# Attention scores as whole float32 products on 64x64 tiles of TensorE, with keys and queries unsplit

## The chip, the cores and the metric

One core of a Trainium2 chip runs the whole program. The metric is the device time of one execution in microseconds; the kernel before was run three times (667.96, 668.06 and 671.06, median 668.06). Lower is better. A profile of one execution lies beside the times; all rows in this document come from such profiles.

## The reference

Four batches of eight heads, 768 tokens, head size 64. Each query attends to the 31 keys around it (distance under 16) and to 24 summaries, one for each block of 32 tokens: of the keys the maximum, of the values the mean. A block's score gets log(32) added. Then comes a feed-forward layer over all heads' outputs. Inputs and outputs are float32 (the weights arrive as 8-byte floats).

```python
k_sum = k.reshape(B, H, nb, 32, D).max(axis=3)
v_sum = v.reshape(B, H, nb, 32, D).mean(axis=3)
scores_l = np.where(abs(i - j) < 16, q @ k.T / 8, -1e9)
scores_s = q @ k_sum.T / 8 + np.log(32)
a = softmax(concat([scores_l, scores_s]))
x = a @ concat([v, v_sum])            # then (tokens, 512)
h = x @ w_in                          # (512, 2048)
out = (h - np.tanh(h)) @ w_out        # (2048, 512)
```

## The kernel before

The work is cut into eight **passes** u = 0 to 7: half a batch's sequence each, 384 queries of all eight heads. Within a pass heads go in four **pairs** p, and the 384 queries in three **tiles** of 128. The attention of a pass feeds its feed-forward part: `moe_in` (line 1071, tiles pH, 12 matmuls for each of 16 slices f of the hidden size) and `moe_out` (line 1136, tiles pY0 to pY2). Both split float32 into a high and a low float32r part and use three matmuls for one; only `moe_out` of pass 0 uses whole float32. A loop over slots (from line 1185 on) lists the steps of all stages: attention runs 22 slots ahead of the feed-forward part, so scores of a later pass stand between pH and pY steps of the one before.

What is listed there is not the order that runs. Each step is a task with a cost for each engine that could take it, the tiles it reads and writes, and a due time; a planner (`schedule`, line 172) simulates the engines and writes one fixed order for each. The tables BIAS, KB and SL move due times by hand. Where the planner sees TensorE idle in the first 100 us it puts dummy matmuls on the identity matrix (`keep_warm`, line 1279, tile pX).

Scores before (`prep` line 781, `scores` line 926):
- Passes 0 and 1 load q and k in rows of 64 numbers, turn them on TensorE (three transposes of q, four of k, in even passes two more for the rest of the keys: "q turn", "k turn", "top turn"), copy them into a line that holds each tile's keys with the 24 block maxima between them, and multiply in whole float32. One half of q per head stands in rows that are zero for the other head, so a tile is four matmuls of 128 rows by 64 columns of the array, 118 columns each (24 summaries and 94 keys), two of them on the left and two on the right half of the array's columns.
- Passes 2 to 7 load q and k as 32x32 blocks, turn them on DVE, split both into high and low parts ("q high", "q low", "q again", "k high", "k low", "k again", "top put"), and make a tile with three float32r matmuls over the whole array:

```python
tensor.matmul(o, at(qh)[:, qs], at(kx[1])[:, :, ws], start=True, stop=False)
for a in range(2):
    tensor.matmul(o[:, a], at(qa[a])[:, qs], at(kx[0])[:, a, ws], start=False, stop=a == 1)
```

After the scores come, tile by tile, a minimum with the mask added ("min", DVE), exponentials (ACT), sums and inverses (DVE) and the scaling; the probabilities are turned (on TensorE in passes 0 and 1, "p turn"; on DVE and through a scratch tensor in the others) and multiplied with the values ("values", 118 rows). Weights come from DRAM into three places of `raw` and are made into float32 on ACT, DVE and POOL (`convert`, line 564). After pass 0 the w_out weights are split too (`split_whole`, line 617) into tiles whose earlier use has ended (`homes`, line 490).

In the trace a float32 matmul stands as two instructions, a float32r matmul and a transpose as one; so a row of a timeline says x4 for two float32 matmuls of the order.

Of the kernel before, what the change touches and what calls it, by code (L numbers as in the profile page):

```python
# [31 lines left out]
WHOLE = 2  # L32

WIDE = 2

MASKED = 0

# [5 lines left out]

KB = {('chunk load', 0): -1261, ('chunk load', 2): 12, ('chunk sum', 0): 636, ('chunk sum', 2): 272, ('const', 0): 183, ('const', 2): -383, ('exp', 0): 297, ('exp', 1): 82, ('exp', 2): -892, ('g', 0): 113, ('g', 1): 66, ('g', 2): 493, ('g high', 1): -379, ('g high', 2): -2162, ('g low', 1): 208, ('g low', 2): 450, ('in', 0): 83, ('in', 1): 8, ('in', 2): -53, ('in part', 2): 226, ('inverse', 0): -566, ('inverse', 1): 1, ('inverse', 2): 770, ('k again', 1): -661, ('k again', 2): -3493, ('k high', 0): 72, ('k high', 1): -374, ('k high', 2): 27, ('k line', 2): -53, ('k load', 0): 397, ('k load', 1): -478, ('k load', 2): 1488, ('k low', 1): -538, ('k low', 2): 636, ('k turn', 0): 300, ('k turn', 1): 34, ('k turn', 2): -325, ('mask split', 2): 129, ('mean copy', 0): 194, ('mean out', 0): -352, ('mean out', 1): -301, ('mean out', 2): -105, ('mean put', 0): 21, ('mean put', 1): 858, ('mean put', 2): 1756, ('mean turn', 0): 376, ('mean turn', 1): -106, ('mean turn', 2): -121, ('min', 0): -122, ('min', 1): 10, ('min', 2): -569, ('normal', 0): 892, ('normal', 1): 313, ('normal', 2): -714, ('out', 0): -471, ('out', 1): -414, ('out', 2): 232, ('p load', 2): 753, ('p out', 0): -129, ('p out', 1): -250, ('p out', 2): 11, ('p save', 2): 740, ('p turn', 0): 40, ('p turn', 1): -180, ('p turn', 2): -212, ('pad', 2): -517, ('pad line', 2): -248, ('pair', 2): 767, ('q again', 1): 38, ('q again', 2): -982, ('q half', 2): -38, ('q high', 0): 669, ('q high', 1): 151, ('q high', 2): -623, ('q load', 0): -366, ('q load', 1): -882, ('q load', 2): 224, ('q low', 1): -548, ('q low', 2): -1311, ('q turn', 0): 656, ('q turn', 1): 183, ('q turn', 2): 51, ('scores', 0): -77, ('scores', 1): -60, ('scores', 2): -6, ('seen', 2): 2487, ('seen max', 2): 1706, ('seen turn', 2): 2079, ('series', 0): 493, ('series', 1): 269, ('series', 2): 349, ('square', 0): 337, ('square', 1): 369, ('square', 2): -674, ('sum', 0): 506, ('sum guard', 0): -45, ('sum guard', 1): -677, ('sum guard', 2): 572, ('tanh', 0): 284, ('tanh', 1): -121, ('tanh', 2): -2026, ('top high', 1): -46, ('top high', 2): -83, ('top line', 2): -207, ('top low', 0): -194, ('top low', 1): -1742, ('top low', 2): -16, ('top max', 0): 144, ('top max', 1): -1138, ('top max', 2): -179, ('top put', 0): -72, ('top put', 1): -846, ('top put', 2): 1034, ('top turn', 0): 154, ('top turn', 1): 15, ('top turn', 2): -3, ('v load', 0): 442, ('v load', 1): -277, ('v load', 2): 100, ('values', 0): -7, ('values', 1): 332, ('values', 2): 456, ('w high part', 0): -51, ('w high part', 1): -1591, ('w high part 2', 0): 399, ('w high part 2', 1): -325, ('w high part 2', 2): -1898, ('w join', 0): 115, ('w join', 1): -38, ('w join', 2): -129, ('w load', 0): 82, ('w load', 1): 468, ('w low', 0): 305, ('w low', 1): -1539, ('w low part', 0): -737, ('w low part', 1): -253, ('w low part 2', 1): -210, ('w low part 2', 2): -1956, ('w scale', 0): 312, ('w scale', 1): -761, ('w sign', 0): 121, ('w sign', 1): -283, ('w sign', 2): -119, ('x high', 0): 248, ('x high', 1): -248, ('x high', 2): 502, ('x low', 0): -591, ('x low', 1): 232, ('x low', 2): 259, ('y out', 2): -505, ('y store', 2): 1285, ('x whole', 2): 34, ('pick', 2): 18, ('big', 1): -123, ('direct', 1): 24, ('cube', 2): -140, ('w shift', 0): -153, ('sum out', 0): -33, ('big', 2): 18, ('top pre', 0): 17, ('pick', 1): -55, ('pick', 0): 21, ('direct', 0): -139, ('cube', 0): 30, ('cube', 1): -7, ('big', 0): 97, ('w sign 2', 0): 34, ('w sign 2', 1): 17, ('w shift', 1): -15}

HALF = {'const': (12, 12), 'k load': (8, 16), 'v load': (18, 36), 'chunk load': (8, 8), 'chunk sum': (8, 8), 'q load': (12, 15), 'w load': (9, 32), 'w scale': (8, 32), 'w shift': (8, 32), 'w low': (7, 32), 'w sign': (3, 20), 'w join': (3, 20), 'w high part': (3, 26), 'w low part': (3, 26), 'w sign 1': (4, 12), 'w sign 2': (4, 12), 'top pre': (16, 16), 'top turn': (4, 8), 'top max': (8, 16), 'top put': (14, 20), 'q turn': (6, 9), 'k turn': (6, 9), 'q high': (4, 8), 'k high': (8, 16), 'sum': (8, 8), 'sum out': (8, 8), 'scores': (17, 25), 'mean turn': (2, 4), 'mean out': (2, 4), 'mean copy': (8, 8), 'mean put': (0, 10), 'min': (32, 50), 'exp': (32, 50), 'sum guard': (15, 25), 'inverse': (15, 25), 'normal': (30, 49), 'p turn': (15, 24), 'p out': (15, 24), 'values': (14, 24), 'x high': (4, 8), 'x low': (4, 8), 'top high': (0, 4), 'top low': (0, 4), 'in': (3, 19), 'tanh': (2, 18), 'square': (3, 18), 'cube': (2, 18), 'series': (2, 18), 'g': (2, 17), 'big': (2, 17), 'direct': (2, 17), 'pick': (2, 17), 'out': (2, 45), 'w high part 2': (3, 6), 'w low part 2': (0, 6), 'g high': (0, 11), 'g low': (0, 10), 'q low': (0, 2), 'q again': (0, 2), 'k low': (0, 2), 'k again': (0, 2), 'y out': (0, 0), 'y store': (0, 0)}


def phase(t):
# [27 lines left out]
HELD = {"pair", "mean copy", "w join", "w shift", "w low", "w sign", "w low part", "w low part 2", "w low part 3", "w high part", "w high part 2", "w scale", "normal", "g high", "g low", "q low", "k low", "g", "cube", "big", "k again", "q again", "top pre"}  # L77
HELD_LATE = {"q high", "k high"}


def holds(t):
    return t.kind in HELD or t.kind in HELD_LATE and phase(t) == 2

# [238 lines left out]
def program(  # L322
# [24 lines left out]
    NG = H // HG  # L347
    PG = HG // 2
    WIN = 15
    SC = 64 + NB + 94  # L350
    N2 = SC - 64
    KS = P + NB
    KC = 3 * KS + P
# [647 lines left out]
    def transpose_probs(u, p, i, tag):  # L1001
# [16 lines left out]
        if i < NT - 1:  # L1018
            return
# [301 lines left out]
```

## Time and profile before

| | |
|---|---|
| median of three runs | 668.06 us (667.96 to 671.06) |
| profiled execution | span 667.8 us, from the first to the last instruction; the list of runs has no separate time for it |
| granted TensorE clock, mean | 0.998 |
| PE, DVE, ACT, POOL busy | 654.8, 473.4, 459.8, 266.7 us |
| DMA | 73.09 MB, mean 109 GB/s |

The page gives busy time by engine and 40 slices of the span; the windows give the same for chosen stretches; a timeline lists instructions of one engine by start. A matmul's shown length contains the time in which it drains, so what a step costs is read from start to start.

### The profile page before, as it was taken

How to read it: one execution, taken by the hardware profiler on the slowest of the kernel's cores; microseconds unless marked ns; L12 is line 12 of the kernel's file. 1: busy time of each engine (PE TensorE's matmuls, PEld its weight loads, DVE VectorE, ACT ScalarE, POOL GpSimd, SP SyncE). 2: the span in 40 equal slices, each digit the busy share in tenths (PEclk: the TensorE clock that was granted, in tenths of full speed). 3: DMA queues.
4: the chain of work that ended last, by engine and by line, in shares of the span. 5: the costliest groups of instructions: out<-in, count | busy, mean ns of one | idle time of the engine just before them, and what ended most of it. 6: DMA issues, size and time to landing. Idle time of an engine off the chain costs nothing.

```text
span 667.8 us, 13029 instructions
## 1 busy us (share of the span) xinstructions
PE 654.8 (98%) x4109; PEld 564.3 (84%) x4109; DVE 473.4 (71%) x1414; ACT 459.8 (69%) x1342; POOL 266.7 (40%) x354
## 2 busy tenths in 40 slices
PE   8999999999999999999999999999999999999997
PEld 6775665788998989899988988898998989898995
DVE  3998889899998889549876799678785875222222
ACT  4997899878885878557883878667765875343332
POOL 4334133146543565335542444544433642122221
PEclk9999999999999999999999999999999999999999
DMA  9897866663245655334244745534252413200001
GB/s 210 231 265 208 216 188 204 144 105 96 71 90 121 151 124 119 76 80 119 60 101 95 161 95 108 121 76 112 60 127 45 108 48 80 61 16 32 1 0 51
DMA packets 165393, 73.09 MB, mean 109 GB/s; under 512 B 131048, under 2 KB 155592, under 8 KB 165320
## 3 DMA queue, kind: packets, MB, share of 16 engines
q1 hardware_dynamic: 164520, 72.02, 44.6%
q8 instruction: 34, 0.56, 0.4%
q10 hardware_dynamic: 800, 0.20, 0.2%
q14 instruction: 39, 0.32, 0.2%
HBM read 54.39 MB, written 15.73 MB: 105 GB/s over the span
## 4 chain that ended last, share of the span: by engine, by line
PE 81%; DVE 8%; ACT 4%; DMA 3%; issue 1%; POOL 0%; SPq 0%; ACTq 0%; DVEq 0%
PE pY L69 37%; PE pH L69 36%; PE pS L69 4%; PE pX L69 2%; PE pT L69 2%; DMA raw<-in_moe_w_out_dram 2%; DVE raw L69 1%; DVE probw L69 1%; DVE k L69 1%; ACT probw L69 1%; ACT gu L69 1%; DMA tmp<-in_v_dram 1%; DVE wf L69 1%; DMA rawq<-in_q_dram 1%; DVE vacc L69 1%
## 5 line engine op out<-in xcount | busy, mean ns | idle before, releaser
L69 PE MATMUL pH<-xh,w 128*128 128x384 f32 x1024 | 268.4, 343 | 0.7 <-POOL w L69 0.5
L69 POOL TENSOR_TENSOR gu<-gu,gt 128x384 f32<-128x384 f32 x112 | 118.1, 1054 | 234.7 <-ACT gu L69 161.6
L69 PEld LDWEIGHTS pH<-xh,w 128*128 128x128 f32 x1024 | 185.7, 188 | 12.5 <-issue 3.3
L69 PE MATMUL pY<-wf,gh 128*128 128x512 f32 x411 | 169.1, 442 | 1.1 <-DVE gh L69 1.1
L69 PE MATMUL pH<-xl,w 128*128 128x384 f32 x448 | 151.8, 339 | 0.0
L69 ACT ACTIVATE gu<-pH 128x384 f32<-128x384 f32 x128 | 62.5, 488 | 106.7 <-PE pH L69 62.7
L69 ACT ACTIVATE prob<-prob,stats 128x182 f32<-128x182 f32 x217 | 93.3, 442 | 36.3 <-DVE stats L69 33.6
L69 PEld LDWEIGHTS pY<-wf,gh 128*128 128x128 f32 x411 | 76.4, 189 | 25.6 <-issue 14.0
L69 DVE CAST gh<-gu 128x384 fp32r<-128x384 f32 x60 | 25.6, 426 | 84.7 <-POOL gu L69 78.6
L69 PEld LDWEIGHTS pH<-xl,w 128*128 128x128 f32 x448 | 84.1, 188 | 0.0
L69 POOL TENSOR_TENSOR gl<-gu,gh 128x384 fp32r<-128x384 f32 x59 | 63.7, 1082 | 35.7 <-DVE gh L69 13.0
L69 ACT ACTIVATE gu<-gu 128x384 f32<-128x384 f32 x128 | 66.9, 522 | 0.5
L69 ACT ACTIVATE gt<-pH 128x384 f32<-128x384 f32 x128 | 61.5, 481 | 2.2 <-PE pH L69 1.9
L69 DVE CUSTOM_DVE_ANT_0 prob<-pS,mask 128x182 f32<-128x182 f32 x144 | 47.1, 340 | 10.5 <-PE pS L69 8.4
L69 PE MATMUL pY<-vsum,gh 128*128 128x512 f32 x126 | 50.1, 398 | 0.0
L69 PE MATMUL pY<-vsum,gl 128*128 128x512 f32 x126 | 49.8, 395 | 0.0
L69 DVE TENSOR_TENSOR k<-raw,k 64x384 fp32r<-64x384 f32 x96 | 46.4, 522 | 1.0
L69 DVE STREAM_TRANSPOSE turned<-prob 128x384 f32<-128x384 f32 x72 | 41.3, 573 | 5.8 <-ACT prob L69 4.5
L69 PE MATMUL pS<-k,q 128*128 128x364 f32 (+1 forms) x208 | 37.8, 295 | 0.9 <-DVE stats L69 0.4
L69 PEld LDWEIGHTS pS<-k,q 128*128 128x128 f32 (+1 forms) x208 | 29.4, 173 | 9.3 <-issue 4.0
L69 DVE TENSOR_TENSOR gl<-gu,gh 128x384 fp32r<-128x384 f32 x53 | 31.2, 589 | 7.0 <-ACT gh L69 3.4
L69 DVE TENSOR_SCALAR raw<-raw 128x512 uint32<-128x512 uint32 (+1 forms) x53 | 33.1, 648 | 3.3 <-DMA raw<-in_moe_w_in_dram 1.9
(185 smaller groups left out, 1185.2 us busy)
## 6 DMA issues: line engine op xcount, KB each, us to landing
place<-turned SPq DMA_DIRECT2D x96, 96.0 KB
probT<-place SPq DMA_DIRECT2D x24, 384.0 KB
raw<-in_moe_w_in_dram SPq DMA_DIRECT2D x16, 512.0 KB
raw<-in_moe_w_out_dram SPq DMA_DIRECT2D x16, 512.0 KB
out_dram<-tmp SPq DMA_DIRECT2D x23, 256.0 KB
rawq<-in_q_dram SPq DMA_DIRECT2D x96, 48.0 KB
raw<-in_k_dram SPq DMA_DIRECT2D x48, 96.0 KB
vw<-in_v_dram SPq DMA_DIRECT2D x40, 96.0 KB
```

What stands on the lines that cost most here:

```text
L69: return lambda *args, **kwargs: self._tc.keep_in_program_order(op(*args, **kwargs))
```

## The change

Scores of all passes become whole float32 products of the unsplit q and k, on quarters of the array: 64 rows (one head of the pair) by 64 columns (one half of a tile's queries). A pair's three tiles are now one step of 24 matmuls, for each tile four on the 24 summaries and four on the 94 keys around (79 at the sequence's ends); head 0 goes to bank pS, head 1 to pT (pY0 in pass 0). The scale -1/8 moves into the "min", masked places get the opposite sign, and the softmax of a pair is one step. In the value tiles the means now stand in rows 0 to 23 and the values behind them.

For that k of batch 0 is loaded in rows of six tokens and q of pass 0 in rows of three. Turning a pair's keys takes 24 transposes on two row halves (once for both passes, kept in a new tile kT), and q of pass 0 six. All steps that split q and k or put summaries between keys are gone, and with them the zero fills and pads. `homes` starts with kT (six split weights), then rawq1, vw1, vsum1 and vsum0. The tables that move due times are new, so nearly every step stands elsewhere.

The core of the diff:

```diff
     def load_k(b, g):
...
-        for h in range(HG):
-            dma("k load", lambda e, h=h: e.dma_start(tile()[:, :, h], k[b, HG * g + h].rearrange("(c r) d -> r c d", c=6)), S * D * 4, D * 4, w=[keys[h]])
+        for m in range(PG):
+            hs = slice(HG * g + 2 * m, HG * g + 2 * m + 2)
+            dma("k load", lambda e, m=m, hs=hs: e.dma_start(at(base)[:, 2 * m:2 * m + 2], k[b, hs].rearrange("h (r c) d -> r h (c d)", c=6)), 2 * S * D * 4, 1536, w=[keys[m]])
...
+        def turn_pair(to, x, n, rows):
+
+            for a in (1, 0):
+                for c in range(n):
+                    for half, o in enumerate(to):
+                        lo = D * (n * (2 * m + a) + c)
+                        tensor.transpose(o[:, c] if a else o[:D, c], x[rows[half], lo - D * a:lo + D], ident[rows[half], rows[half]])
...
+        do("k turn", PE, 1.05, turn_k, r=[k_keys[m], IDENT], w=[(x, 0) for x in pk])
...
-            tensor.matmul(o, at(qh)[:, qs], at(kx[1])[:, :, ws], start=True, stop=False)
-            for a in range(2):
-                tensor.matmul(o[:, a], at(qa[a])[:, qs], at(kx[0])[:, a, ws], start=False, stop=a == 1)
...
+        def go():
+            for i in range(NT):
+                for near in range(2):
+                    for a in range(2):
+                        for half in range(2):
+                            rows, x = slice(64 * a, 64 * a + 64), P * i + 64 * half
+                            first = t0 + x - WIN
+                            lo, hi = max(first, 0), min(first + NK, S)
+                            w = k_all()[rows, lo:hi] if near else at(top)[rows, NB * m:NB * (m + 1)]
+                            c = N2 * i + (NB + lo - first if near else 0)
+                            tensor.matmul(at(ss[a])[64 * half:64 * half + 64, c:c + (hi - lo if near else NB)], q_all()[rows, x:x + 64], w, start=True, stop=True)
...
-    homes, late = {}, 5
-    for tag, bufs, n in (("vsum0", 1, 3), ("vsum1", 1, 3), ("probw", 3, 1), ("rawq1", 1, 2), ("vw1", 1, 3)):
...
+    homes, late = {}, 1
+    for tag, n in (("kT", 6), ("rawq1", 2), ("vw1", 3), ("vsum1", 3), ("vsum0", 2)):
...
-            either("k high", k_cost, lambda e, a=a: highs(e, a), r=kr, w=[(kx[0], a)])
-            if len(kx) > 1:
-                do("k low", DVE, 0.69, lambda a=a: lows(a), r=[*kr, (kx[0], a)], w=[(kx[1], a)])
```

Three places show how the order moves. On TensorE in pass 2, before, one tile's scores among steps of the feed-forward part of the pass before (k and q are the split keys and queries, qa one head's low part):

```order
L69 MATMUL pY_1874<-vw_1619,gh 128x512
L69 MATMUL pY_1874<-wf_2619,gh 128x512
L69 MATMUL pY_1874<-vw_1619,gl 128x512
L69 MATMUL pS<-k_1455,q_1296 128x364
L69 MATMUL pS<-k_1292,q_1471 128x182
L69 MATMUL pS<-k_1292,qa 128x182
L69 MATMUL pH<-xh,w_79 128x384 x2
```

The same place now, the first of three tiles of a pair's scores (top holds the summaries, raw the turned keys, rawq the turned queries):

```order
L65 MATMUL pY_1875<-rawq_1333,gh 128x512
L65 MATMUL pY_1875<-wf_1789,gh 128x512
L65 MATMUL pY_1875<-rawq_1333,gl 128x512
L65 MATMUL pS<-top_1883,rawq_96 64x24 x2
L65 MATMUL pT<-top_1883,rawq_96 64x24 x2
L65 MATMUL pS<-raw,rawq_96 64x79
L65 MATMUL pS<-raw,rawq_96 64x94
L65 MATMUL pT<-raw,rawq_96 64x79
L65 MATMUL pT<-raw,rawq_96 64x94
```

Three matmuls became eight, and the two other tiles follow directly; before, each tile stood by itself between pH and pY steps.

On SP, the program's first transfers, before (xl is k's tile, vw the value tiles, xh the values for the means):

```order
L69 DMA xl<-in_k_dram 128x6x64 x3
L69 DMA rawq_98<-in_q_dram 128x3x64
L69 DMA xl<-in_k_dram 128x6x64
L69 DMA vw_100<-in_v_dram 16x4x64
L69 DMA xl<-in_k_dram 128x6x64
L69 DMA xh<-in_v_dram 128x4x384
L69 DMA rawq_98<-in_q_dram 128x3x64
L69 DMA vw_100<-in_v_dram 96x4x64
```

and now:

```order
L65 DMA rawq_108<-in_q_dram 128x2x192
L65 DMA xl<-in_k_dram 128x2x384
L65 DMA vw_128<-in_v_dram 16x4x64
L65 DMA rawq_96<-in_q_dram 128x2x192
L65 DMA xl<-in_k_dram 128x2x384 x2
L65 DMA xh<-in_v_dram 128x4x384 x2
L65 DMA raw<-in_moe_w_in_dram 128x4x256
```

One transfer now brings two heads, both means' values come ahead of most value rows, and the first weights (raw) stand ninth on the queue, where they were 26th.

On TensorE, one pair's tile of pass 0 before:

```order
L69 MATMUL pY_197<-k_116,q_119 64x118 x2
L69 MATMUL pY_197<-k_116 64x118 x2
L69 MATMUL pS<-k_116,q_119 64x118 x2
L69 MATMUL pS<-k_116 64x118 x2
L69 MATMUL pT<-ident,xl 128x128 x2
```

and the start of a pair's scores of pass 0 now, behind the dummies:

```order
L65 MATMUL pX<-ident 128x128 x3
L65 MATMUL pS<-top_183,q_155 64x24 x2
L65 MATMUL pY_205<-top_183,q_155 64x24 x2
L65 MATMUL pS<-kT,q_155 64x79
L65 MATMUL pS<-kT,q_155 64x94
L65 MATMUL pY_205<-kT,q_155 64x79
L65 MATMUL pY_205<-kT,q_155 64x94
```

Before, pY and pS take turns from tile to tile; now each holds one head's scores of all three tiles.

## Rows read from the trace of the kernel before

**Rows 1.** The page: busy time, and busy tenths in 40 slices, PE and DVE.
```profile
PE 654.8 (98%) x4109; PEld 564.3 (84%) x4109; DVE 473.4 (71%) x1414; ACT 459.8 (69%) x1342; POOL 266.7 (40%) x354
...
PE   8999999999999999999999999999999999999997
...
DVE  3998889899998889549876799678785875222222
```
**Rows 2.** Windows: stretch, its length, busy us of engines, PEclk, DMA share, GB/s.
```profile
0.00:10.00 10.00, 7.30 (x37) 6.81 (x39) 1.87 (x9) 2.85 (x5) 5.40 (x27) 1.00 0.99 208
...
30.00:40.00 10.00, 9.08 (x103) 7.20 (x101) 8.56 (x32) 9.54 (x30) 5.47 (x5) 1.00 0.84 240
...
90.00:100.00 10.00, 10.00 (x71) 6.13 (x72) 7.08 (x25) 8.79 (x18) 2.74 (x2) 1.00 0.80 232
...
150.00:250.00 100.00, 99.86 (x600) 89.96 (x599) 89.03 (x265) 78.51 (x238) 54.14 (x75) 1.00 0.47 109
```
**Rows 3.** Groups by line and shape, PE: busy us, mean ns, idle before and releasers.
```profile
L69 PE MATMUL pX<-ident 128*128 128x128 f32 x76 | 13.0, 320 | 2.0 <-POOL ident L69 1.5 <-ACT xh L69 0.4
```
**Rows 4.** Timeline of PE, 213 us: start, length, instruction, count.
```profile
212.96 0.40 PE L69 MATMUL pY<-vw,gl 128*128 128x512 f32 x1
213.20 0.41 PE L69 MATMUL pS<-k,q 128*128 128x364 f32 x2
...
213.56 0.54 PE L69 MATMUL pH<-xh,w 128*128 128x384 f32 x2
213.94 0.34 PE L69 MATMUL pH<-xl,w 128*128 128x384 f32 x1
```
**Rows 5.** Timeline of PE, 17 us, two float32 tiles of scores in pass 0.
```profile
17.16 0.37 PE L69 MATMUL pY<-k,q 128*64 128x118 f32 x4
17.37 0.37 PE L69 MATMUL pY<-k 128*64 128x118 f32 x4
```
**Rows 6.** Timeline of PE, 117 us, turning of probabilities.
```profile
116.76 0.22 PE L69 MATMUL pT<-ident,probw 64*118 64x64 f32 x1
116.76 0.22 PE L69 MATMUL pS<-ident,probw 64*118 64x64 f32 x1
116.82 0.22 PE L69 MATMUL pT<-ident,probw 64*118 64x64 f32 x1
```
**Rows 7.** Timeline of PE, 104 us, a float32 tile of pass 1 between pH steps.
```profile
104.09 0.51 PE L69 MATMUL pH<-xh,w 128*128 128x384 f32 x2
104.44 0.33 PE L69 MATMUL pH<-vsum,w 128*128 128x384 f32 x1
104.69 0.42 PE L69 MATMUL pS<-k,q 128*64 128x118 f32 x4
...
105.25 0.62 PE L69 MATMUL pH<-xh,w 128*128 128x384 f32 x2
...
105.88 0.52 PE L69 MATMUL pH<-xh,w 128*128 128x384 f32 x2
```
**Rows 8.** Timeline of PE, 71 us, k turn of a pair of pass 1.
```profile
70.96 0.60 PE L69 MATMUL pS<-ident,xl 128*128 128x128 f32 x4
71.39 1.02 PE L69 MATMUL pY<-wf,gh 128*128 128x512 f32 x2
```
**Rows 9.** Timeline of SP's queue: first issue of weights.
```profile
19.94 0.39 SPq L69 DMA_DIRECT2D raw<-in_moe_w_in_dram  x1
```
**Rows 10.** Groups by line and shape, ACT, 0 to 60 us: copies of keys.
```profile
L69 ACT ACTIVATE k<-pH 128x384 f32<-128x384 f32 x4 | 2.0, 488 | 0.9 <-DVE th L69 0.6 <-PE pH L69 0.3
...
L69 ACT ACTIVATE k<-pH 128x49 f32<-128x49 f32 x4 | 0.8, 206 | 0.0
```
**Rows 11.** The page: costliest groups, two of DVE.
```profile
L69 DVE CUSTOM_DVE_ANT_0 prob<-pS,mask 128x182 f32<-128x182 f32 x144 | 47.1, 340 | 10.5 <-PE pS L69 8.4
...
L69 DVE TENSOR_TENSOR k<-raw,k 64x384 fp32r<-64x384 f32 x96 | 46.4, 522 | 1.0
```
**Rows 12.** One tile's instructions, 150 to 660 us, tile k: count, ns, first and last start.
```profile
L69 PEld LDWEIGHTS pS<-k,q x140: 186/188/189, 151.4 to 562.2; 128*128 128x128 f32 x140
```

More of the change, by code (lines that the diff above doesn't have):

```diff
@@ L747, in put_mean @@
     def put_mean(u, g):
         vw = vw_of(u, g)
-        for half in range(2):
-            r = 64 * (1 - half)
-            keys = [vw_keys(vw, i, half)[2] for i in range(NT)]
-            def to(r=r, half=half):
-                return at(vw)[r:r + NB, :, half].rearrange("r i h d -> r i (h d)")
-            x = mean[32 * g:32 * g + NB].unsqueeze(1).broadcast_to([NB, NT, HG * D])
-            if u < 1:
-                either("mean copy", {DVE: 0.66, ACT: 0.86}, lambda e, to=to, x=x: copy(e, to(), x), r=[MEAN[g]], w=keys)
-            else:
-                dma("mean put", lambda e, to=to, x=x: e.dma_start(to(), x), NT * NB * HG * D * 4, 1024, r=[MEAN[g]], w=keys)
@@ new lines, in put_mean @@
+        x = mean[32 * g:32 * g + NB].unsqueeze(1)
+        if u < 1:
+            for half in range(2):
+                either("mean copy", {DVE: 0.66, ACT: 0.86}, lambda e, half=half: copy(e, at(vw)[:NB, :, half].rearrange("r i h d -> r i (h d)"), x.broadcast_to([NB, NT, HG * D])), r=[MEAN[g]], w=[vw_keys(vw, i, half)[2] for i in range(NT)])
+            return
+        dma("mean put", lambda e: e.dma_start(at(vw)[:NB].rearrange("r i f h d -> r (i f) (h d)"), x.broadcast_to([NB, 2 * NT, HG * D])), 2 * NT * NB * HG * D * 4, 1024, r=[MEAN[g]], w=[vw_keys(vw, i, half)[2] for i in range(NT) for half in range(2)])
@@ new lines, in tops, with largest, scores @@
+    def tops(b, p):
+        base = ("top", b, p // PG)
+        if base not in made_by:
+            buf(base, f"top{p // PG}", [P, PG * NB])
+        return base, p % PG
+    def largest(top, x, n, blocks):
+        n += NB * top[1]
+        vector.tensor_reduce(at(top[0])[:, n:n + blocks], x.rearrange("p (n t) -> p n t", t=32), axis=AX.X, op=ALU.max)
+    def scores(u, p, tags):
+        ss, b, t0 = [bank(("s", u, p, a), tags[a]) for a in range(2)], u // 2, U * (u % 2)
+        top, m = tops(b, p)
@@ L904, in prep_sums @@
-    def prep_sums(u, p):
-        _, kx = operands(u, p)
-        tops, keys, col = top_of[u // 2, p]
-        def put(e, j, a):
-            rows = slice(64 * a, 64 * a + 64)
-            x = at(kx[j]).bitcast(F32)[rows, a, P:]
-            to = bass.AP(tensor=x.tensor, offset=x.offset, ap=[list(x.ap[0]), [KS, NT], [1, NB]])
-            if u >= WHOLE:
-                to = to.bitcast(F32R)
-            copy(e, to, at(tops[j])[rows, col:col + NB].bitcast(F32).unsqueeze(1).broadcast_to([64, NT, NB]))
-        if u < WHOLE:
-            def line(e):
-                x = at(kx[0])[:, 0, P:]
-                to = bass.AP(tensor=x.tensor, offset=x.offset, ap=[list(x.ap[0]), [KS, NT], [1, NB]])
-                copy(e, to, at(tops[0])[:, col:col + NB].bitcast(F32).unsqueeze(1).broadcast_to([P, NT, NB]))
-            either("top line", {POOL: 0.3, DVE: 0.21, ACT: 0.25}, line, r=keys[0], w=[(kx[0], "sums0")])
-            return
-        for a in range(2):
-            for j in range(len(kx)):
-                either("top put", {POOL: 0.3, DVE: 0.21, ACT: 0.25}, lambda e, j=j, a=a: put(e, j, a), r=keys[j], w=[(kx[j], "sums%d" % a)])
@@ L1037, in values @@
     def values(u, p, tag):
-        pairs = [p - 1, p] if u >= WIDE else [p]
+        pairs = [p - 1, p] if u >= WHOLE else [p]
         for x in pairs:
@@ L1257, in program @@
                             load_k_blocks(b, p - PG + 1 + n)
-            else:
-                scores(*s0, tag_s)
+        if s is not None and s[2] == NT - 1 and (s[0] < WHOLE or s[1] % PG == PG - 1):
+            values(*s[:2], ("pX", "pY2")[s[1] % 2] if s[0] == 0 else "pX")
+            for p in range(s[1] - PG + 1 if s[0] >= WHOLE else s[1], s[1] + 1):
+                x_split(s[0], p)
+            if s[:2] == (0, 0):
+                sum_means(0, 1, "pX")
         if B > 1 and j in (20, 28):
```

452 lines of the change are left out of this document (150 added, 302 removed).

## The prediction

> **What bounds the kernel now.** I read the page first, then the stages, then TensorE's timeline around single steps. PE is busy for 98% of the span, and from the middle on the slices stand at 9 while DVE falls to 2 [rows 1]. The windows tell the stages apart [rows 2]. In 150 to 250 us PE is busy for 99.86 us of 100, at a granted clock of 1.00 (the 2.4 GHz level), so there a microsecond of PE work is a microsecond of time. In the first 10 us PE is busy for only 7.30 and the DMA share is 0.99; at 30 to 40 us ACT is busy for 9.54 of 10, DVE for 8.56, and PE's 9.08 are not all useful: the 76 dummy matmuls on `ident`, which the planner puts where PE would stand still, make up 13.0 us [rows 3]. So the head is set by loads and by DVE and ACT, and the rest by the sum of PE's work. The sum below is made against the profiled span of 667.8; the median of the runs, 668.06, is 0.26 more.
>
> **Scores of passes 2 to 7 (72 tiles, 24 pairs).** Before, a tile is three matmuls over the whole array. It starts at 213.20 and the next step at 213.56: 0.36 us; the pY ahead of it takes 0.24 (512 columns at 2.4 GHz are 0.21) and the first two pH after it 0.38 (twice the usual 0.18 is 0.36), so I put 0.04 for its edges [rows 4, 7]. 0.40 x 72 = 28.8 us, 1.20 a pair.
>
> After, a pair is one burst of 24 float32 matmuls on quadrants of the array. No row shows four quadrants at work, so I build it from three things that rows do show.
> - *Rounds.* The old float32 tiles of passes 0 and 1 use two column halves at once. Each of their matmuls stands twice in the trace (x4 where the order has x2), and x4, two rounds of two, take 17.37 - 17.16 = 0.21, so 0.10 a round of 118 columns [rows 5]. Two row halves run together as well: the transposes of p into pT and pS start at the same 116.76, the next two at 116.82, 0.06 a round of 64 columns [rows 6]. With both splits together, a pair is 12 rounds of four instructions: six of 94 columns (some of 79), 0.10 x 94/118 = 0.08 each, and six of 24 columns. For these 0.02 would follow from the columns; I take 0.06, the shortest round that a row shows. 6 x (0.08 + 0.06) = 0.84 us.
> - *Edges of a burst.* The float32 tile at 104.69 has four rounds, 0.40. But the pH ahead of it starts 0.25 earlier (0.18 is its usual step), the tile takes 0.56 to the next start, and the next three pH take 0.63 (usually 0.54) [rows 7]. In all 0.07 + 0.56 + 0.09 = 0.72, so 0.32 for going into the small tiles and out of them. The old f32r tile has only 0.04 of it; the new burst pays it once a pair.
> - *Sum.* 0.84 + 0.32 = 1.16 a pair, 27.8 for 24: **-1.0 us**. The ends: with 0.02 for the short rounds 0.60 + 0.32 = 0.92, which is -6.7; if only two quadrants ever run at once, 1.68 + 0.32 = 2.00, which is +19.2. I stay near the middle since column halves and row halves are each shown at work.
>
> **Scores and turns of pass 1.** Twelve tiles at 0.72 are 8.6; four bursts at 1.16 are 4.6: -4.0 (ends -4.9 and -0.6). Its k turns go, since kT now holds the turned keys of the whole batch: four times four transposes, 70.96 to 71.39, 0.43 each [rows 8]: -1.7. The stage still waits now and then for converted weights, so of -5.7 I count four fifths: **-4.5 us**.
>
> **The head (pass 0).** PE's part is nearly even there. Per pair the k turn grows from six transposes to 24 (12 rounds of 0.06, so 0.7, plus edges, against 0.43 and half of it again for the top turn), the q turn from three to six; the scores shrink from 3 x 0.72 to 1.16. That is a PE with dummies in it, so I count nothing for either: what covers it are the loads, DVE and ACT. If that cover went, it would cost or give under a microsecond a pair.
> What does count: (a) Loads. K of batch 0 and q of pass 0 are 16 heads' pieces, 1.57 + 0.79 MB by the shapes in the code, read until now in runs of 256 bytes, then in 1536 and 768. In the first 10 us the engines move 208 GB/s at a share of 0.99, in 90 to 100 us, where the weights' long runs dominate, 232 at 0.80, which would be 290 at full share [rows 2]. 2.36 MB are 11.2 us at the one and 8.1 at the other: 3.1 us less of a full DMA. On SP's queue four k and three q issues fewer stand ahead of the weights, the first of which was issued only at 19.94, as SP's 26th [rows 9]; by the order it is now the ninth. (b) Copies. By the shapes a pair of pass 0 keeps its copies but for one q half against one k half, and loses the 0.21 for a key line's edge; a pair of pass 1 loses a key line (0.49 + 0.21) and one q half (384 columns too, 0.49): 1.2 us, the short line of block tops not counted [rows 10]. Over four pairs each that is 5.6 us from DVE and ACT together, 2.8 each. (a) and (b) run side by side, and the rest of the chain (exps, values, x, first weights) stays: **-2.5 us**, between 0 and -5.
>
> **At nothing.** In passes 2 to 7 the splitting of q and k on DVE, ACT and POOL goes; its largest group alone is 46.4 us of DVE [rows 11]. PE at 99.86 of 100 hides it already, so it gives nothing. The p turn on DVE (one for three), the merged mean puts and the new homes of split weights are off PE too. What could go late instead: a burst needs pS and pT free, so the six mins of the pair before must be through. Pairs come every 17 us (bursts from 151.4 to 562.2, 24 of them [rows 12]); six mins of 0.34 on DVE are some 2 us [rows 11]. The first six split weights now live in kT, free only after the last scores of pass 1; by the order several pY and pH steps lie between.
>
> **Sum.** -1.0 - 4.5 - 2.5 = -8.0: a span of 659.8, a measured time of **660**.
>
> **Rivals.**
> 1. *All four quadrants overlap fully, and the head gives all it can.* A short round then takes half of what I put, 0.03: 0.66 + 0.32 = 0.98 a pair, -5.3 for 24, 0.8 x (-4.7 - 1.7) = -5.1 of pass 1, -4.5 for the head: 653. For it: within a round the starts in rows 6 coincide to the hundredth. Against: no row has a round under 0.06. The Trainium skill ("TensorE: Matmul & The Clock Gate", Part 3) gives a pack of tiles the time of one matmul and about 4 ns per further tile; by that, an estimate, a round of four is longer by 12 ns and this rival holds. Chance 0.20.
> 2. *TensorE cannot start the many small instructions faster.* The burst is 48 instructions in the trace's count where nine stood. The densest stream in the rows is two per 0.06 us, so 0.029 each. If that is the instructions' own floor rather than the columns' time, a pair takes 48 x 0.029 = 1.39 + 0.32 = 1.71: 24 x (1.71 - 1.20) = +12.2, pass 1 only 0.8 x (-1.8 - 1.7) = -2.8, the head -2.5. That is +6.9, so 675. It decides where a pair takes over 1.45 us, at which the parts cancel. For it: with 64 columns the two floors can't be told apart. Against: starts of a round coincide, so the instructions are not spaced evenly. The same page (Part 1) says that starts of matmuls never come closer than about 25 ns however few the columns; by that, an estimate, a pair is 1.2 + 0.32 = 1.52 and the kernel some 670. The coinciding starts in rows 6 speak against it for different tiles, and no run here shows it for four. Chance 0.13.
> 3. *No change.* The head's savings only lengthen dummies, pass 1's become waits for weights (ACT at 9.54 of 10 feeds them too), and 24 x 0.04 is left: 667. For it: PE has dummies and idle time in the head [rows 2, 3], and the order still has 36 dummies of before's 38. Against: from 60 us on nearly every slice of PE stands at 9 [rows 1]. Chance 0.14.
>
> **Numbers.** The forecast has 0.53. Its own range, from the ends of the head and of pass 1 and a burst between 1.0 and 1.3 us, is 655 to 665. For 8 times in 10 I reach down to 651, past rival 1, and up to 670, past rival 3 and into the lower part of rival 2. A measurement of this kernel can tell about 0.5%, 3.3 us, from no change: the forecast and rival 1 are faster, 0.73; rival 3 is the same, 0.14; rival 2 is slower, 0.13.
>
> **What would show it.** Right: in the timeline of the changed kernel a burst that costs between 1.0 and 1.3 us with its edges, short rounds near 0.06; the first matmul on weights some microseconds earlier than before; no wait over 1 us between 150 us and the end. Wrong: bursts over 1.5 us (rival 2), or bursts as I say with dummies and waits for weights grown by as much as the scores shrank (rival 3). A wait at the first pY on kT, or at a burst for DVE's mins, would be a cost I left out.

## The result and the profile after

The changed kernel takes **661.88 us** (median of 4 runs, 660.97 to 663.39); the kernel before, run on the same chip, 668.28. The ratio is 0.9902 (95% interval 0.9881 to 0.9924): faster by 1.0%, some 6.5 us. Timed again beside the last experiments it stood at 0.9886 (0.9868 to 0.9904). The forecast was 660, its range 651 to 670.

The page of the changed kernel (busy time, and busy tenths of PE and DVE in 40 slices), to be laid beside [rows 1]:

```profile
span 660.3 us, 14416 instructions
...
PE 646.4 (98%) x5301; PEld 550.2 (83%) x5301; DVE 331.1 (50%) x1070; ACT 390.1 (59%) x1166; POOL 186.9 (28%) x190
...
PE   8999999999999999999999999999999999999995
...
DVE  4898898998745675435454543314332433111111
```

DVE lost 142 us of work, ACT 70, POOL 80, and PE only 8.4. The span fell by 7.5, which is about what PE lost: the splitting was hidden, as [rows 1, 2] had it. In the windows of the stages (columns as in [rows 2]) the loads fill less of the DMA in the first 10 us (share 0.78, before 0.99), and PE is full to the last hundredth from 150 to 250 us:

```profile
0.00:10.00 10.00, 7.86 (x82) 6.68 (x86) 2.23 (x6) 2.24 (x3) 2.83 (x17) 1.00 0.78 262
...
30.00:40.00 10.00, 9.00 (x164) 6.99 (x159) 9.18 (x35) 9.96 (x32) 2.78 (x2) 1.00 0.87 245
90.00:100.00 10.00, 10.00 (x83) 6.12 (x82) 9.02 (x32) 9.73 (x29) 2.16 (x2) 1.00 1.03 259
150.00:250.00 100.00, 100.00 (x925) 87.78 (x924) 65.62 (x221) 58.68 (x201) 35.50 (x34) 1.00 0.58 131
```

Now a burst, in PE's timeline at 317 us (start, length, instruction, count), which stands where [rows 4] had a float32r tile:

```profile
316.65 0.39 PE L65 MATMUL pY<-kT,gl 128*128 128x512 f32 x1
316.97 0.24 PE L65 MATMUL pS<-top,rawq 64*64 64x24 f32 x2
316.98 0.24 PE L65 MATMUL pT<-top,rawq 64*64 64x24 f32 x2
...
317.30 0.19 PE L65 MATMUL pS<-top,rawq 64*64 64x24 f32 x2
317.31 0.19 PE L65 MATMUL pT<-top,rawq 64*64 64x24 f32 x2
...
317.57 0.19 PE L65 MATMUL pS<-top,rawq 64*64 64x24 f32 x2
...
317.96 0.63 PE L65 MATMUL pH<-xh,w 128*128 128x384 f32 x2
318.42 0.34 PE L65 MATMUL pH<-xl,w 128*128 128x384 f32 x1
```

From 316.97 to 317.96 are 0.99 us for 48 instructions. The middle tile, 317.30 to 317.57, takes 0.28 for 16 of them: two short rounds and two long ones. The price of a burst with its edges I take as the time from the start of the step before it to the start of the third step behind it, less the usual 0.18 of a pH and 0.23 of a pY: 1.19 us, the median of the 22 bursts after 150 us, which all stand between such steps. By the same rule an old tile after 150 us took 0.39 by the median (0.394) and 0.41 by the mean, because two of 60 tiles came late (those at 162.4 and 399.0 us): 1.18 to 1.23 a pair.

TensorE's last matmul starts 10.6 us earlier than before, at 652.10 where it was 662.73. But the span is only 7.5 shorter. The end of the timeline shows why; first the kernel before:

```profile
655.92 0.27 PE L69 MATMUL pT<-ident,stats 128*1 128x128 f32 x1
656.23 0.28 DVE L69 TENSOR_REDUCE seen<-pT 1x1 f32<-1x128 f32 x1 [0.55 <-PE pT L69]
661.77 0.60 ACT L69 ACTIVATE tmp<-pY 128x512 f32<-128x512 f32 x1 [5.61 <-PE pY L69]
662.40 0.34 SPq L69 DMA_DIRECT2D out_dram<-tmp  x1
...
662.73 0.40 PE L69 MATMUL pY<-vw,gl 128*128 128x512 f32 x1
...
663.16 0.60 ACT L69 ACTIVATE tmp<-pY 128x512 f32<-128x512 f32 x1
663.78 0.33 SPq L69 DMA_DIRECT2D out_dram<-tmp  x1
```

and the changed kernel:

```profile
651.87 0.39 PE L65 MATMUL pY<-vsum,gl 128*128 128x512 f32 x1
652.10 0.27 PE L65 MATMUL pT<-ident,stats 128*1 128x128 f32 x1
652.41 0.28 DVE L65 TENSOR_REDUCE seen<-pT 1x1 f32<-1x128 f32 x1 [4.16 <-PE pT L65]
653.27 0.60 ACT L65 ACTIVATE qa<-pY 128x512 f32<-128x512 f32 x1 [4.40 <-DVE seen L65]
653.77 1.08 ACT L65 ACTIVATE tmp<-pY 128x512 f32<-128x512 f32 x2
653.89 0.34 SPq L65 DMA_DIRECT2D out_dram<-qa  x1
654.38 1.62 SPq L65 DMA_DIRECT2D out_dram<-tmp  x2
```

The check of the sums (`seen`) decides at a branch whether the whole program is done again, and the last three y outs stand behind that branch. Before, its turn ran 6.8 us ahead of PE's last step, and each y out followed its own pY. Now the turn is PE's very last instruction, ACT is idle for 4.40 us until `seen`, and then does three y outs in a row. From PE's last start to the end of the span it takes 8.2 us where it was 5.1. **These 3.1 us are a loss that the change brought with it.** It has two parts: up to the end of ACT's last y out it is 2.75 us where it was 1.03, from there to the end of the span 5.45 where it was 4.04. The first, 1.7 more, is the wait for the check; the second, 1.4 more, stands behind the y outs.

### The profile page after: what moved, and what is told of

It reads as the page before. It is cut to its first block, busy times and chain, and to the rows that moved or that the text cites. A ratio compares the mean times of both kernels' runs of the same rounds, so it can differ in the third digit from the quotient of the medians.

```text
span 660.3 us, 14416 instructions
## 1 busy us (share of the span) xinstructions
PE 646.4 (98%) x5301; PEld 550.2 (83%) x5301; DVE 331.1 (50%) x1070; ACT 390.1 (59%) x1166; POOL 186.9 (28%) x190
## 4 chain that ended last, share of the span: by engine, by line
PE 87%; DMA 5%; DVE 3%; ACT 2%; SPq 1%; issue 1%; POOL 0%; ACTq 0%; DVEq 0%
PE pY L65 39%; PE pH L65 39%; PE pS L65 3%; PE pT L65 3%; PE pX L65 2%; DMA xl<-in_k_dram 2%; DMA raw<-in_moe_w_out_dram 1%; SPq L65 1%; DMA tmp<-in_v_dram 1%; DMA raw<-in_moe_w_in_dram 1%; ACT tmp L65 1%; ACT raw L65 1%; DVE prob L65 1%; DVE tmp L65 0%; DVE raw L65 0%
## 5 line engine op out<-in xcount | busy, mean ns | idle before, releaser
L65 POOL TENSOR_TENSOR gl<-gu,gh 128x384 fp32r<-128x384 f32 x112 | 114.2, 1020 | 253.0 <-ACT gh L65 232.7
L65 DVE TENSOR_TENSOR gu<-gu,gt 128x384 f32<-128x384 f32 x72 | 40.9, 568 | 218.7 <-ACT gu L65 199.8
L65 ACT ACTIVATE gh<-gu 128x384 fp32r<-128x384 f32 x109 | 57.2, 525 | 72.6 <-DVE gu L65 40.1
L65 ACT ACTIVATE prob<-prob,stats 128x118 f32<-128x118 f32 x207 | 78.2, 385 | 14.2 <-DVE stats L65 14.1
L65 POOL TENSOR_TENSOR gu<-gu,gt 128x384 f32<-128x384 f32 x40 | 41.3, 1031 | 119.0 <-ACT gu L65 113.6
L65 PE MATMUL pY<-kT,gh 128*128 128x512 f32 x126 | 50.4, 400 | 0.0
L65 PE MATMUL pY<-kT,gl 128*128 128x512 f32 x126 | 49.6, 394 | 0.3 <-POOL gl L65 0.3
L65 DVE TENSOR_SCALAR prob<-prob,stats 128x118 f32<-128x118 f32 x177 | 49.3, 344 | 0.8
L65 ACT ACTIVATION_READ_ACCUMULATOR prob<-prob,stats 128x1 f32 x192 | 36.5, 190 | 0.0
L65 DVE CUSTOM_DVE_ANT_0 prob<-pS,mask 128x118 f32<-128x118 f32 x96 | 25.4, 277 | 17.5 <-PE pT L65 16.2
```

The costliest lines, as they stand in the source:

```text
L65: return lambda *args, **kwargs: self._tc.keep_in_program_order(op(*args, **kwargs))
```

## The experiments

Every ratio is to the kernel before on the same chip; 0.01 of it is 6.7 us. Where the changed kernel was not timed beside an experiment, I read it against 0.9894, the mean of its own two ratios.

**Heads apart.** Do the four quadrants work together?

```diff
-            for i in range(NT):
-                for near in range(2):
-                    for a in range(2):
+            for a in range(2):
+                for i in range(NT):
+                    for near in range(2):
```

> The changed kernel with the same 24 matmuls of a burst in another order: all of the pair's first head (rows 0 to 63 of the array), then all of the second (rows 64 to 127). Only two quadrants, the two column halves, can then be at work at a time; the number of instructions is the same. Theory that the four quadrants run together: the rounds double from 12 to 24, and a pair grows by the 0.84 us of the forecast's rounds, from 1.19 to about 2.0: 24 x 0.84 = +20 us in passes 2 to 7 and up to +6 in passes 0 and 1, so 680 to 688, slower than the kernel before. Rival, the instructions are what takes the time (48 of them at 17 ns is the same 0.84): no change, 661 to 663.

Measured: 677.7, ratio 1.0114 (1.0079 to 1.0149), 14.7 us above the changed kernel. In PE's timeline a burst:

```profile
302.12 0.36 PE L65 MATMUL pS<-raw,rawq 64*64 64x79 f32 x4
302.29 0.27 PE L65 MATMUL pS<-top,rawq 64*64 64x24 f32 x4
302.38 0.38 PE L65 MATMUL pS<-raw,rawq 64*64 64x94 f32 x4
302.57 0.24 PE L65 MATMUL pS<-top,rawq 64*64 64x24 f32 x3
302.61 0.24 PE L65 MATMUL pT<-top,rawq 64*64 64x24 f32 x2
```

A tile of one head, 302.29 to 302.57, takes 0.28 for 8 instructions: as long as 16 on four quadrants. So two row halves run fully side by side, and it is not the count of instructions that takes the time. The burst costs 1.79 with its edges, 0.61 more, not 0.84, because the second head starts (302.61) before the first is through. 24 x 0.61 = 14.6 is as much as the whole growth, whose interval reaches 2 us to either side; that passes 0 and 1 add little is likely, not shown.

**Short rounds twice, and 64 columns instead.** What sets the length of a short round?

```diff
-                for near in range(2):
+                for near in (0, 0, 1):
```

> The changed kernel with every short matmul of the scores (64 by 24 columns, on the block tops) issued twice in a row with the same operands and output: a burst is 36 float32 matmuls, 72 instructions in the trace's count, instead of 24 and 48. Nothing else is moved. Theory of rounds (four quadrants at work together, a round lasts as long as its columns take): a pair gets six more rounds of 24 columns. In the trace of the changed kernel the steady tile takes 0.28 us for 16 instructions; by the forecast's split a short round is 0.06, by the starts seen in that trace about 0.035. So +0.2 to +0.36 us for each of 32 pairs: +6.5 to +11.5 us, 24 of them fully in the part that TensorE bounds, so 667 to 673. Rival, a floor per instruction: 24 more instructions a pair at 0.025 to 0.029 us is +0.6 to +0.7 a pair, +19 to +22 us in all, 681 to 684. Other rival, short matmuls hidden altogether behind the long ones of other quadrants: 662 to 664.

Measured: 672.21, ratio 1.0039 (1.0021 to 1.0056), 9.7 us above the changed kernel. A tile in the middle of a burst:

```profile
300.23 0.18 PE L65 MATMUL pS<-top,rawq 64*64 64x24 f32 x1
...
300.35 0.21 PE L65 MATMUL pS<-top,rawq 64*64 64x24 f32 x1
...
300.62 0.18 PE L65 MATMUL pS<-top,rawq 64*64 64x24 f32 x1
...
```

The tile takes 0.39 (300.23 to 300.62), 0.117 more than the 0.278 without the two added rounds: 0.058 a round. A pair grows from 1.19 to 1.54, that is 0.35 for six rounds. If the tile's own short rounds take 0.058 too, (0.278 - 2 x 0.058) / 2 = 0.081 is left for a long one. These are the 0.06 and 0.08 of the forecast. The loads of the weights (LDWEIGHTS, PEld's rows) show the same beat in the middle tile of the changed kernel, one load a round:

```profile
317.30 0.14 PEld L65 LDWEIGHTS pS<-top,rawq 64*64 64x64 f32 x2
...
317.35 0.14 PEld L65 LDWEIGHTS pS<-raw,rawq 64*64 64x64 f32 x2
...
317.41 0.14 PEld L65 LDWEIGHTS pS<-raw,rawq 64*64 64x64 f32 x2
...
317.50 0.14 PEld L65 LDWEIGHTS pS<-top,rawq 64*64 64x64 f32 x2
...
317.58 0.14 PEld L65 LDWEIGHTS pS<-top,rawq 64*64 64x64 f32 x2
```

Two gaps of 0.05 to 0.06 and two of 0.08 to 0.09.

The second run puts a matmul of 64 columns of keys where the first had a second one of 24:

```diff
-                for near in range(2):
+                for near in (-1, 0, 1):
...
-                            w = k_all()[rows, lo:hi] if near else at(top)[rows, NB * m:NB * (m + 1)]
+                            w = k_all()[rows, lo:lo + 64] if near < 0 else k_all()[rows, lo:hi] if near else at(top)[rows, NB * m:NB * (m + 1)]
```

> The changed kernel with one more float32 matmul on 64 columns of keys ahead of each short one (same queries, its output overwritten by the two that follow): a burst is 36 matmuls, as in the run with the short ones twice, but the extra ones have 64 columns, not 24. That run took 0.35 us more for a pair, 0.058 for each added round of four. Theory: up to 64 columns a round takes the same 0.058 (the transposes of 64 columns show 0.058 too), it is the floor of one instruction on its quadrant and no longer the columns: a pair 0.35 more, 672 again. Rival, the columns' time counts even here: 94 columns are 0.081 by the old tile's 0.10 for 118, 64 would be 0.055 and 24 only 0.02, and the 0.35 of the other run came from something else; then this run is above that one by 6 x 0.035 x 32 = 6.7 us, 679.

Measured: 671.09, ratio 1.0018 (1.0004 to 1.0031). A pair costs 1.54 in its trace, the same as with 24 columns. From 24 to 64 columns a float32 round takes one and the same 0.058: a floor. Whether it is the matmul's own or that of the load of its weights, these runs do not settle; for the load speaks that the floor is 0.058 with weights of 64 columns and 0.112 with weights of 128 (the dummies of the next experiment).

**A burst in three pieces.** What do the edges cost? Two dummies of 32 columns in each burst, either between its tiles or behind it:

```diff
             for i in range(NT):
+                if i:
+                    tensor.matmul(px_bank[:, 512 - P:512 - P + 32], ident, ident[:, :32], start=True, stop=True)
```

> The changed kernel with each burst cut in three: between its three tiles stands a dummy matmul on the whole array (ident by 32 columns of ident, into the spare columns of pX), two a pair. To be read against the next run, which has the same two dummies behind the burst. Theory of the forecast (0.32 us for going from the large matmuls into the small tiles and out again, paid once a pair; 0.35 in the trace of the changed kernel): the two extra entries and exits cost 2 x 0.35 = 0.7 a pair over the next run, 24 x 0.7 = +17 us in passes 2 to 7 and up to +5 in passes 0 and 1; 683 to 690 as a whole. Rival, the edges are something of the burst's first matmuls alone (a late operand, the change of type): no difference to the next run beyond 2 us.

```diff
                             tensor.matmul(at(ss[a])[64 * half:64 * half + 64, ...
+            for i in range(2):
+                tensor.matmul(px_bank[:, 512 - P:512 - P + 32], ident, ident[:, :32], start=True, stop=True)
```

> The changed kernel with the two dummies of the run before, both behind the burst, so that the burst stays whole. A dummy of 128 columns starts 0.22 us after the one before it in the trace (two instructions of 0.11); one of 32 columns is 0.05 to 0.12. So +0.1 to +0.25 a pair: 24 pairs +2.5 to +6, and something for passes 0 and 1; 664.5 to 670. It is the base that the run before is read against.

Measured: 689.5 (ratio 1.0300, 1.0273 to 1.0326) in between, 673.98 (1.0062, 1.0038 to 1.0086) behind: 15.9 us apart. In the traces a burst with its dummies costs 2.19 and 1.63, so two more cuts are 0.55, 0.28 each, a little under the 0.35 that the whole burst pays. The edge is paid at each change between the full array and its quadrants, and joining a pair's three tiles into one burst saves two of them. The dummies are float32 as the scores are, so the change of type alone does not make it: the rival falls. The second of these expectations was wrong: the dummies behind the burst cost 0.45 a pair, not 0.1 to 0.25.

```profile
301.43 0.63 PE L65 MATMUL pX<-ident 128*128 128x32 f32 x4
301.89 0.47 PE L65 MATMUL pY<-kT,gh 128*128 128x512 f32 x1
```

Four instructions from 301.43 to 301.89 are 0.115 each with the step into them, and 0.112 from the second on; the dummies of 128 columns start 0.112 apart too. A quarter of the columns saved nothing.

**Old run lengths.** Part (a) of the head.

```diff
-            dma("k load", lambda e, m=m, hs=hs: e.dma_start(at(base)[:, 2 * m:2 * m + 2], k[b, hs].rearrange("h (r c) d -> r h (c d)", c=6)), ...
+            dma("k load", lambda e, m=m, hs=hs: [e.dma_start(at(base)[:, 2 * m + a].rearrange("p (c d) -> p c d", c=6), k[b, HG * g + 2 * m + a].rearrange("(c r) d -> r c d", c=6)) for a in range(2)], ...
```

(and the same for the queries of pass 0)

> The changed kernel with the keys of batch 0 and the queries of pass 0 loaded as the kernel before did: one DMA for each head, in runs of 256 bytes, where the changed kernel has one for two heads in runs of 1536 and 768. The rows then stand in another order in the buffer, so the output is another one; the work, the order and the bytes are the same. Theory of the forecast, part (a) of the head: 2.36 MB took 11.2 us of the DMA engines at the old rate and 8.1 at the new, so up to 3.1 us come back, and the first matmul on weights is later by about as much: 663.5 to 665. Rival: the head is held by DVE's and ACT's copies and by TensorE, not by these loads (the first matmul on weights came 1.9 us later with the change, not earlier): 661.5 to 662.5.

Measured: 664.86, ratio 0.9936 (0.9914 to 0.9958), 2.8 us above the changed kernel, as expected of (a); some 2 without the three of its twelve executions that took 667.7 to 669.3, at a granted clock of 0.989 to 0.992. In the first 10 us the engines move 176 GB/s at a share of 0.95 where the changed kernel moves 262 at 0.78:

```profile
0.00:10.00 10.00, 6.60 (x45) 5.56 (x46) 1.67 (x5) 2.15 (x3) 2.82 (x17) 1.00 0.95 176
```

The first matmul on weights starts at 36.37 in this trace, which is one of those three executions. So the loads do count at the start. The edit undoes the length of the runs and the number of transfers at once (the first weights are issued at 9.21, not 5.04); which of the two costs more is not told apart.

**Copies twice.** Part (b) of the head.

```diff
-lambda e: copy(e, at(qf)..., at(pq)...)
+lambda e: [copy(e, at(qf)..., at(pq)...) for n in range(2)]
```

(and the same for k out)

> The changed kernel with each copy of turned queries and keys out of PSUM in passes 0 and 1 (q out, k out: 16 of some 0.48 us, on DVE or ACT) done twice in a row, 7.7 us more for DVE and ACT together. Theory of the forecast, part (b) of the head: these two engines bound the head, 5.6 us of copies less were worth half of it, so the time grows by about half of the 7.7, +3 to +4 us: 665 to 666. Rival: the loads (part (a)) and TensorE bound the head, and the copies lie beside them: 662 to 663.

Measured: 665.31, ratio 0.9931 (0.9907 to 0.9955), 2.5 us above the changed kernel for 7.7 us of copies, about a third; in the trace TensorE's steps from 48 us on are 2.8 us later, from 109 us 3.6 to 3.8, at the end 3.2. Copies and loads both lie on the way to the end of the head.

**More turns in pass 1.**

```diff
                 tensor.transpose(at(pq)[:, P * i:P * (i + 1)], ...
+            for i in range(8):
+                tensor.transpose(at(pq)[:, U:U + P], q_rows(rawq)[:, i % NT, hs].rearrange("p a d -> p (a d)"), ident)
```

> The changed kernel with eight more transposes of 128 by 128 behind the q turn of each pair of pass 1 (into spare columns of the same bank, read by no one): twice the old k turn of that pass, which took 0.43 us a pair. 4 x 0.86 = 3.4 us of TensorE work in pass 1. Theory of the forecast: pass 1 is bound by TensorE for four fifths, so +2.8 us against the changed kernel run beside it. Rival: pass 1 waits for converted weights anyway, the work fills holes: 0 to +1. Other rival, fully bound: +3.4.

Measured: 663.19, ratio 0.9920 (0.9895 to 0.9945), beside 662.08 and 0.9886 (0.9868 to 0.9904) for the changed kernel. That is 2.3 us by the ratios and 1.1 by the medians, for 3.4 us of work, and the intervals overlap. Two of the six executions took 666.4 and 667.0, at a granted clock of 0.992 and 0.991; the other four took 662.3 to 663.4, where the changed kernel takes 661.5 to 663.4. The trace has the 129th matmul of `moe_in` 2.5 us later than the changed kernel's second profile (99.39, 96.93), but the 193rd only 0.5 (131.10, 130.61), and PE's last start no later at all (652.17, 652.64). From 100 to 150 us, first with the turns, then without:

```profile
100.00:150.00 50.00, 50.00 (x397) 36.77 (x396) 46.49 (x115) 37.42 (x101) 13.57 (x13) 1.00 0.63 144
...
100.00:150.00 50.00, 49.15 (x393) 36.02 (x393) 47.46 (x112) 36.36 (x98) 12.81 (x12) 1.00 0.60 136
```

So in pass 1 the work does cost time, but much of it goes into time that PE would have lost further on. The four fifths of the forecast are not shown; the rival of 0 to +1 fits the trace better.

**Keeping the clock.** In the profiled execution of the changed kernel the granted clock fell to 0.5 (1.2 GHz) at 25.9 us, after PE had stood still for two stretches of 0.8 us.

```diff
+        if small_only and getattr(t, "name", None) == ("sum", 1):
+            for n in range(4):
+                keep_warm()
```

> The changed kernel with four more dummy matmuls on ident in front of the sum of the second half's values (sum 1, pX<-xh,vacc). In the trace of the changed kernel TensorE stands still from 23.1 to 24.1 us and from 24.9 to 25.85, and the granted clock is 0.5 from 25.9 to 29.3; the first matmul on weights starts at 31.4, 1.9 us later than before the change. Theory: the second of these holes costs the clock, and the clock costs half of 3.4 us; with the hole filled (4 x 0.21 us) the clock stays at 1.00, the first matmul on weights comes 1.5 to 1.9 us earlier, and so does all behind it: 660 to 660.5. Rival 1: the clock falls all the same, from the first hole: 662. Rival 2: the clock stays, but the weights are not there earlier, so the gain is eaten by waits: 661 to 662.

Measured: 662.64, ratio 0.9905 (0.9881 to 0.9929): no gain. Windows of 20 to 30 us, first the changed kernel as first profiled,

```profile
20.00:30.00 10.00, 8.39 (x121) 5.69 (x122) 7.76 (x36) 7.42 (x26) 0.00 (x0) 0.83 0.99 270
```

then with the dummies,

```profile
20.00:30.00 10.00, 8.83 (x147) 6.95 (x146) 8.07 (x39) 8.25 (x29) 0.31 (x1) 1.00 0.89 235
```

and last the changed kernel in its second profile,

> The changed kernel itself, timed again beside the three other runs of this call, as the base that they are read against. On this chip it should stand at 0.988 to 0.992 of the kernel before, as at first.

measured at 662.08, ratio 0.9886 (0.9868 to 0.9904), where the same window reads

```profile
20.00:30.00 10.00, 8.70 (x164) 6.87 (x163) 8.64 (x41) 9.27 (x33) 0.35 (x1) 1.00 0.95 264
```

With the dummies the clock stayed at 1.00, but so it did without them in the second profile. There the first matmul on weights starts at 29.90, not 31.38, and the span is 660.7: no shorter. Its lead, still 1.3 us at the 129th matmul of `moe_in` (96.93 against 98.23), is gone at the 193rd (130.61 against 130.45). Nor is the fall an accident of one execution: it stands at the same holes in the profiles of the check first (26.4 us) and of the old run lengths (27.9 us), but not in most others, where the first hole was mostly shorter (0.5 us in the second profile). The changed kernel's execution with the fall took 662.02, its others beside it 660.97 to 663.39; but the executions at a mean clock of 0.992 or less, named above, were 3 to 5 us longer than others of their kernel. Whether the clock is the cause there, or a late start that lowers it, was not tested.

**The check first.** What does the end cost?

```diff
+        for t in tasks:
+            if t.kind in ("seen", "seen turn", "seen max"):
+                t.level += 5000
```

> The changed kernel, with one thing moved: the planner is told to place the check of the sums of squares ('seen', its turn on TensorE, 'seen max') as soon as its inputs are there. On TensorE the turn pT<-ident,stats then stands some twenty pY matmuls before the last one, not behind it; all else keeps its order. Theory: in the changed kernel the last TensorE matmul starts 10.6 us earlier than before (662.7 to 652.1), but from there to the end of the span it takes 8.2 us where before it took 5.1, because the three last y outs on ACT stand behind the branch, which waits for this check, which waits for a turn that TensorE does after its last pY. Then the end comes some 3 us earlier: about 659 against 662 of the changed kernel, ratio to the kernel before 0.985 to 0.987, and the three output DMAs are issued one by one, each after its own pY. Rival: the 8.2 us are the last DMAs themselves, or the branch costs the same wherever it stands; then 661 to 662, ratio 0.990.

Measured: 661.1, ratio 0.9857 (0.9827 to 0.9887), 2.5 us below the changed kernel. With the four dummies of the run before added to it:

> The early check of the sums and the four dummies in front of sum 1, together: two earlier runs gave ratios of 0.986 and 0.9905 for them alone, where the changed kernel had 0.9902. If the early check's 3 us is real, it shows again: about 659, ratio 0.985 to 0.987; the dummies kept the granted clock at 1.00 from 25 to 30 us but brought the first matmul on weights only 0.5 us forward, so no more than 0.5 us from them. Rival, the first figure was luck of that chip: as the changed kernel beside it, within 1 us.

Measured: **659.15**, ratio **0.9843** (0.9826 to 0.9860), the fastest version: 2.9 us under the changed kernel beside it, whose 662.08 gives 0.9886. Its end, in ACT's, SP's and PE's rows:

```profile
651.16 0.60 ACT L65 ACTIVATE qa<-pY 128x512 f32<-128x512 f32 x1 [2.22 <-PE pY L65]
...
651.79 0.34 SPq L65 DMA_DIRECT2D out_dram<-qa  x1
651.85 1.28 ACT L65 ACTIVATE tmp<-pY 128x512 f32<-128x512 f32 x2
...
652.10 0.39 PE L65 MATMUL pY<-vsum,gl 128*128 128x512 f32 x1
652.47 1.15 SPq L65 DMA_DIRECT2D out_dram<-tmp  x2
```

PE's last start is at 652.10 as in the changed kernel; the first y out stands ahead of it, the last ends 1.0 us after it, as before the change, and the span ends at 658.1 where it ended at 660.3. So the wait for the check is gone. But from PE's last start to the end it still takes 6.0, not 5.1: 0.9 us of the loss remain behind the last y out, and no run says why.

## Why the prediction was right, step by step

**Scores of passes 2 to 7: right for the burst, and within about 1 us for the term.** 24 x (1.19 - 1.23) = -1.0 with the old tiles' mean, 24 x (1.19 - 1.18) = +0.2 with their median; -1.0 was forecast. So the bursts gave between nothing and 1 us, and the sign is not shown. The parts of the new burst hold one by one: a short round is 0.058 (I took 0.06), a long one 0.081 (0.08), the edges 1.19 - 0.84 = 0.35 (0.32). Taking the shortest round that a row showed [rows 6], and not the 0.02 that 24 columns would give, was the choice that decided it (0.92 a pair and -6.7 otherwise), and two runs show it. That column halves and row halves work together, which no row had shown at once, is shown by the heads apart. Rival 1's half-length short rounds fall with the doubled ones, and rival 3 with the 10 us that the head and pass 1 gave (below).

**Rival 2 fell.** 16 instructions in 0.28 us are 0.017 each, under its floor of 0.029, and on two quadrants 8 instructions take as long. The Trainium skill ("TensorE: Matmul & The Clock Gate", Part 1) says that starts never come closer than about 25 ns; this trace has the four starts of a round about 7 ns apart, so the rule does not hold across quadrants. Part 3 of the same page of the Trainium skill counts a pack of tiles as one matmul and some 4 ns for each further tile; that a tile takes 0.28 on two quadrants and on four fits a pack that costs hardly more than its longest member.

**Head and pass 1: the sum was too small, and its split is not shown.** Without the end's loss the span would be 10.6 shorter, and passes 2 to 7 have at most 1.0 of that; some 10 are left where I had 4.5 + 2.5 = 7.0. The work of the two stages is interleaved, so the trace does not split it. "(a) and (b) run side by side" made 2.5 us of the head's two parts together. Undone one at a time, (a) costs 2 to 2.8, and (b) a third of the copies' time, which for the 5.6 us that the change took away is 1.8. Together that is some 4 to 4.6, near the end of 5 that I had set; that the two add up also when both are taken away was not tried. Pass 1's four fifths are not shown (the added turns fit a smaller share better). That leaves 5 to 6 us, pass 1's part among them, that no run ascribes. The new tables that move due times are a rival for them: the same work in the old order was not run.

**The first matmul on weights: wrong.** I expected it some microseconds earlier; it started at 31.38 in the one profile and 29.90 in the other, after 29.52 before. The weights themselves were asked for 15 us earlier, at 5.04 instead of 19.94 [rows 9]:

```profile
5.04 0.77 SPq L65 DMA_DIRECT2D raw<-in_moe_w_in_dram  x1
```

The first split weights are ready some 9 us earlier, at 28.77 before

```profile
27.50 1.27 POOL L69 TENSOR_TENSOR w<-qa,w 128x512 fp32r<-128x512 f32 x1
```

and at 19.85 now:

```profile
18.58 1.27 POOL L65 TENSOR_TENSOR w<-qa,w 128x512 fp32r<-128x512 f32 x1 [3.56 <-ACT w L65]
```

Before, the matmul came 0.8 us behind its weights; now it comes 11.5 behind them, so it is no longer the weights that it waits for. It also needs x of the first pair, and ahead of it on PE stand sum 1 and the turns of the next pair. The gain shows behind it: the 49th matmul on weights of pass 0 starts at 55.15, before at 64.16.

**The end: not foreseen.** The list "at nothing" has no word on the check. In the order of the changed kernel `pT<-ident,stats` is PE's last row, behind all pY, and before it was not; with the branch ahead of the last y outs that is a step moved past the last work of the kernel, to be costed like the others. The loss at the end was 3.1 us in the traces; moving the check forward gave back 2.2 of them there, and 2.5 and 2.9 us in two timed runs. The cause of the other 0.9 stays open.

So the forecast of -8.0 against a span 7.5 shorter owes something to luck: some 3 too little in the head and pass 1, and 3.1 of loss left out. "No wait over 1 us between 150 us and the end" held for PE, but the cost sat where PE was done.

## What to carry to other kernels

Before one adds up what a change saves, look at what stands behind the last instruction of the engine that bounds the kernel: a planner that is given new costs may put a small check there, and the end then waits for it. Read the price of the old step by the same rule as that of the new one, and look whether a few late ones make its mean. For a shape that no row shows, take a round of small matmuls as no shorter than the shortest one in the trace, count the four quadrants of a round as one, and pay for each change between small tiles and the full array. A fall of the clock in a single profile is not yet a cause of the time: profile again before mending it.

## What the hardware showed that I had not expected

- A float32 round on quadrants takes 0.058 us at 24 columns and at 64; at 94 it takes 0.081. A tile of both kinds takes 0.28 on two quadrants and on four.
- Cutting a burst of quadrant matmuls with a matmul of the full array costs 0.28 us a cut, both float32.
- A float32 matmul of the full array with 32 columns costs 0.112 for each of its two instructions, as much as one with 128.
- Taking 2.36 MB of loads in runs of 256 bytes and twice as many transfers, instead of runs of 768 and 1536, brought the first 10 us from 262 to 176 GB/s, at a higher DMA share (0.95 against 0.78).
- The same kernel with the same order had a clock of 0.83 on average from 20 to 30 us in one profile and 1.00 in another, and spans of 660.3 and 660.7.
